# A scheduled attention kernel: a clock for the load queue, normalisation on GpSimd, and a later gate exponential

## The chip, the cores and the metric

The kernel runs on one core of a Trainium2 chip. The metric is the device time of one execution in microseconds (us); lower is better. Times are medians of several executions. All executions count as undisturbed ("fast"). Ratios are computed from the mean time of one kernel's fast runs over that of the other's in the same rounds, so they are not quite the ratio of the medians quoted; the 95% interval stands behind them. The kernel before ran again beside every set of experiments and had medians of 902.8, 902.4, 902.3 and 901.9 us.

The engines' names in the profile are: PE (TensorE, matrix products), PEld (its weight loads), ACT (ScalarE), DVE (VectorE), POOL (GpSimd), SP (SyncE, which here issues the loads and stores). L827 is line 827 of the kernel in question; line numbers differ from kernel to kernel.

## The reference, cut to what matters

Two attention blocks are computed and concatenated, each with 32 heads of 16 columns over 2048 positions (bf16).

```python
# A: four segments of 512 positions, each with causal local attention and a memory
for s in range(4):
    p = softmax(q_s @ k_s^T * scale + causal_mask);  a_dot = p @ v_s
    a_mem = (phi(q_s) @ M) / (phi(q_s) @ z + 1e-6)       # phi(t) = t+1 if t>0 else exp(t)
    o_s = g * a_mem + (1 - g) * a_dot                    # g = sigmoid(beta), one per head
    M += phi(k_s)^T @ v_s;  z += sum(phi(k_s))
# B: full attention over 2048 positions
o = softmax(q @ k^T * scale) @ v
# both: o @ wo
```

The exponentials of the softmax dominate. Block B alone has 32 x 2048 x 2048 of them.

## The kernel before: the parts the change touches

The program is written by a scheduler in Python. It keeps a model clock for each engine (`T["pe"]`, `T["act"]` and so on), picks the next piece of work by these clocks, and pins the order that results. At run time every engine follows its own list in that order; a wait that the model did not foresee holds up everything behind it on that engine (in the kernel before, the copy of kA had its input at 9.03 us and started at 13.13, behind an exponential that waited for a load until 13.02).

Scores go in tiles of three and two banks (512 columns each) to ScalarE's exponential. A part of the score quads (a quad is four score tiles of 512 columns) goes to VectorE instead: four *evacuations* out of PSUM (the accumulator memory) into 16-bit integers that are bit patterns of exponentials, then three *rungs*, which shift a whole quad by a constant within SBUF (the on-chip memory).

```python
# evacuation (PSUM -> SBUF) and rung (SBUF -> SBUF), both on VectorE
nc.vector.tensor_scalar(x[:, j, :], vt[:], XSCALE, float(LADDER[0]), ALU.mult, ALU.add)
nc.vector.tensor_scalar(p[:], x[:], float(off - LADDER[0]), 32767.0, ALU.add, ALU.min)
```

A finished pair of heads is normalised on VectorE. `tT` is the transposed local product, `aT` that of the memory.

```python
def fin_pair(wk, st, name, rt, ridx, ot):
    ...                                      # reciprocals of the sums: rr, r2
    t1, t2 = tT[:, :, :, 0:DH], aT[:, :, :, 0:DH]
    yield -0.7
    pin(nc.vector.tensor_tensor(t1, t1, rr.to_broadcast(bc), op=ALU.mult))
    yield -0.7
    pin(nc.vector.tensor_tensor(t2, t2, r2[:].to_broadcast(bc), op=ALU.mult))
    yield -0.7
    pin(nc.vector.tensor_tensor(o, t1, t2, op=ALU.add))
```

The loads and transposes of x (`xT_a`) and of phi(k) (`phk`) stand in one queue on SP. The scheduler guesses when they will have landed:

```python
rel = T["pe"] + 10                      # projections of segment s > 0 not before this
...
held["pk"] = T["dve"] + 6.5
chore(d - 3, mem(), 2, after=T["dve"] + 7)     # memory products after the transposes of phk
```

The head copies the first keys on ScalarE, behind the gate exponential in program order:

```python
pin(nc.scalar.activation(gcol[:], beta_t[:], ACT.Exp, scale=-1.0))   # needs the load of beta
pin(nc.scalar.copy(kA[0, 0][:], ps0[0][:]))                          # the first scores need kA
```

The tail computes four last output tiles (`l_ps`), checks all sums (`flag`; a branch over an exact fallback follows it), and evacuates the output tiles.

## Time and profile before

The kernel took 902.71 us (902.5 to 904.79, three runs); the profiled run took 901.82 with a span of 900.1 us from its first instruction to its last. From the page of the kernel before, first the busy time of the engines, then the costliest groups of ScalarE and VectorE (line, engine, operation, tiles, shapes, count, then busy us and mean ns of one, then idle time just before and its main releaser):

```profile
PE 866.8 (96%) x7674; PEld 260.2 (29%) x7674; DVE 794.2 (88%) x1359; ACT 868.2 (96%) x779; POOL 152.1 (17%) x327
...
L827 ACT ACTIVATE pT<-s_ps 128x1536 bf16<-128x1536 f32 x749 | 856.8, 1287 | 8.3 <-PE s_ps L109 6.1
L899 DVE TENSOR_SCALAR vx<-v_ps 128x512 uint16<-128x512 f32 x496 | 324.7, 684 | 30.2 <-PE v_ps L109 23.8
...
L915 DVE TENSOR_SCALAR vx<-vx 128x2048 uint16<-128x2048 uint16 x372 | 244.6, 690 | 1.9 <-PE acc L109 0.7
```

TensorE and ScalarE are both busy 96% of the span, but a part of TensorE's work adds nothing to the result (411 products with zeros, busy 137.1 us, which the scheduler puts in as *warming* when TensorE has little to do). ScalarE has nothing of the kind, so it is the bound, and the span divides into what stands before, in and behind its row of exponentials. I read these parts from the start and end of every ScalarE instruction in the trace:

| part of the span, kernel before | us |
|---|---|
| until the first exponential starts | 14.41 |
| ScalarE at work until the last exponential ends (1872 banks) | 864.9 |
| ScalarE idle in the first 20 us after its first exponential | 4.4 |
| ScalarE idle later | 3.2 |
| from the end of the last exponential to the end | 13.1 |

The later idle time is almost nil: in the middle only 3.2 us of some 850 are lost. The head is where time is lost openly. The timeline of the kernel before (start, length, engine, line, operation, count, and in brackets the idle time before it and what ended it):

```profile
9.07 1.41 DVE L1069 TENSOR_SCALAR qA<-q_ps,par 128x512 bf16<-128x512 f32 x2 [6.20 <-PE q_ps L109]
...
13.02 0.21 ACT L1066 ACTIVATE gcol<-beta_t 128x8 f32<-128x8 bf16 x1 [9.66 <-DMA beta_t<-in_A_beta_dram]
13.13 0.57 ACT L1067 CAST kA<-k_ps 128x512 bf16<-128x512 f32 x1
...
14.41 2.37 ACT L827 ACTIVATE pT<-s_ps 128x1536 bf16<-128x1536 f32 x2 [0.71 <-PE s_ps L109]
```

The first projections end at 9.03, but the copy of kA waits behind the gate exponential, which waits for beta until 13.02. And the tail, timeline of the kernel before:

```profile
890.84 0.89 DVE L1165 STREAM_TRANSPOSE OT_b<-tN 128x128 bf16<-128x128 bf16 x4
...
891.65 0.14 DVE L420 TENSOR_SCALAR okt<-rsum 128x32 bf16<-128x32 f32 x1
...
891.85 1.07 ACT L1181 CAST osb<-l_ps 128x512 bf16<-128x512 f32 x2 [4.91 <-PE l_ps L109]
...
892.69 0.14 DVE L1175 TENSOR_SCALAR flag<-f_ps 1x1 int32<-1x1 f32 x1 [0.26 <-PE f_ps L109]
892.76 1.29 DVE L1179 CAST osb<-l_ps 128x512 bf16<-128x512 f32 x2
```

The check of sums runs between 891.65 and 892.83; VectorE's output copies come after it.

### The profile page before, as it was taken

Reading aid. Unit: us, or ns where it says so; the run is one execution under the profiler, and the core shown is the slowest. Engines: PE = TensorE matmul, PEld = TensorE weight load, DVE = VectorE, ACT = ScalarE, POOL = GpSimd, SP = SyncE. Lnnn points to the kernel's source line nnn. Section 1 sums busy time; section 2 is a strip of 40 time slices with the busy share of each in tenths; the row PEclk is TensorE's granted clock in tenths of the full one; section 3 lists DMA queues with packets and bytes.
Section 4 is the critical chain, followed back from the end, with each engine's and each line's share of the span. In section 5 each row is a group of like instructions: output and inputs, shape, how many; then the busy total and the mean of one; then the engine's idle time right before and its main releaser. Section 6 shows DMA issues by size and latency. Waiting matters only on the chain.

```text
span 900.1 us, 18954 instructions
## 1 busy us (share of the span) xinstructions
PE 866.8 (96%) x7674; PEld 260.2 (29%) x7674; DVE 794.2 (88%) x1359; ACT 868.2 (96%) x779; POOL 152.1 (17%) x327
## 2 busy tenths in 40 slices
PE   6999999999999999999999999999999999999996
PEld 2222222232323223222232223223222222222321
DVE  1777789989898998988989999999999899999995
ACT  3899999999999999999999999999999999999994
POOL 4630120411303003030120304002030300000000
PEclk8999999999999999999999999999999999999998
DMA  7700000010000110000000010000000000000001
GB/s 185 143 13 7 24 4 5 7 25 7 7 1 14 36 30 8 1 1 7 1 7 2 25 30 1 1 1 1 2 2 1 19 30 1 2 1 2 1 2 28
DMA packets 35649, 15.47 MB, mean 17 GB/s; under 512 B 27360, under 2 KB 35552, under 8 KB 35552
## 3 DMA queue, kind: packets, MB, share of 16 engines
q1 hardware_dynamic: 33776, 13.78, 6.5%
q8 instruction: 62, 1.02, 0.5%
q10 hardware_dynamic: 1776, 0.40, 0.2%
q14 instruction: 35, 0.29, 0.1%
HBM read 4.20 MB, written 4.19 MB: 9 GB/s over the span
## 4 chain that ended last, share of the span: by engine, by line
PE 42%; ACT 31%; issue 12%; DVE 5%; POOL 2%; DVEq 0%; ACTq 0%; POOLq 0%
ACT pT L827 30%; PE acc L109 19%; PE s_ps L109 11%; PE v_ps L109 7%; POOL pT L837 2%; DVE vx L899 2%; PE o_ps L109 2%; PE k_ps L109 1%; DVE vx L915 1%; ACT ex L284 1%; PE q_ps L109 1%; PE am_ps L109 0%; DVE tT L358 0%; DVE tN L391 0%; POOL qB L259 0%
## 5 line engine op out<-in xcount | busy, mean ns | idle before, releaser
L827 ACT ACTIVATE pT<-s_ps 128x1536 bf16<-128x1536 f32 x749 | 856.8, 1287 | 8.3 <-PE s_ps L109 6.1
L899 DVE TENSOR_SCALAR vx<-v_ps 128x512 uint16<-128x512 f32 x496 | 324.7, 684 | 30.2 <-PE v_ps L109 23.8
L109 PE MATMUL s_ps<-qB,KB 32*128 32x512 bf16 x1552 | 250.7, 382 | 8.9 <-ACT pT L827 5.5
L915 DVE TENSOR_SCALAR vx<-vx 128x2048 uint16<-128x2048 uint16 x372 | 244.6, 690 | 1.9 <-PE acc L109 0.7
L109 PE MATMUL acc<-vx,VB 128*32 128x512 f16 x1984 | 181.3, 385 | 0.6 <-DVE vx L915 0.3
L109 PE MATMUL v_ps<-qB,KB 32*128 32x512 bf16 x496 | 171.4, 382 | 1.1 <-DVE vx L899 0.5
L837 POOL TENSOR_SCALAR_AFFINE_SELECT pT<-pT 128x256 bf16<-128x256 bf16 (+2 forms) x242 | 104.8, 462 | 306.0 <-ACT pT L827 304.7
L109 PE MATMUL acc<-pT,VB 128*32 128x512 bf16 x1552 | 152.8, 387 | 0.0
L109 PEld LDWEIGHTS <-KB 32*128 32x128 bf16 x2048 | 84.2, 91 | 235.8 <-issue 227.8
L109 PE MATMUL acc<-zeros 128*128 128x512 bf16 x411 | 137.1, 386 | 0.0
L109 PEld LDWEIGHTS <-VB 128*32 128x32 bf16 x3536 | 74.5, 94 | 161.7 <-issue 152.4
L109 PE MATMUL s_ps<-qA,kA 32*128 32x384 bf16 (+3 forms) x512 | 54.1, 303 | 7.7 <-ACT kA L1067 4.7
L109 PEld LDWEIGHTS <-zeros 128*128 128x128 bf16 x433 | 35.1, 98 | 84.9 <-issue 77.0
L259 POOL TENSOR_SCALAR qA<-qc,par 128x512 bf16<-128x512 bf16 x24 | 16.5, 701 | 248.6 <-DVE qc L257 248.6
L358 DVE STREAM_TRANSPOSE tT<-acc 128x512 f32<-128x512 f32 x64 | 45.0, 704 | 10.2 <-PE acc L109 9.9
L109 PE MATMUL acc<-pT,vA 128*32 128x256 bf16 (+3 forms) x512 | 32.5, 305 | 1.2 <-DVE vx L899 0.8
L109 PEld LDWEIGHTS <-kA 32*128 32x128 bf16 x512 | 17.1, 92 | 47.8 <-issue 39.7
L259 POOL TENSOR_SCALAR qB<-qc,par 128x512 bf16<-128x512 bf16 x32 | 23.6, 750 | 8.6 <-DVE qc L257 8.6
L435 DVE CAST osb<-o_ps 128x512 bf16<-128x512 f32 x28 | 19.2, 687 | 6.6 <-PE o_ps L109 6.3
L304 DVE CAST vA<-v_ps 128x512 bf16<-128x512 f32 x16 | 11.0, 689 | 11.7 <-PE v_ps L109 11.7
L257 DVE CAST qc<-q_ps 128x512 bf16<-128x512 f32 x28 | 19.2, 684 | 2.4 <-PE q_ps L109 2.1
L109 PE MATMUL k_ps<-xT_a,w_a 128*128 128x512 bf16 x64 | 19.6, 383 | 0.8 <-DMA xT_a<-in_A_x_dram 0.7
(88 smaller groups left out, 419.1 us busy)
## 6 DMA issues: line engine op xcount, KB each, us to landing
out_dram<-osb SPq DMA_DIRECT2D x31, 128.0 KB, 1.7
w_b<-in_B_wqkv_dram SPq DMA_DIRECT2D x3, 512.0 KB, 5.2
phk<-phkT SPq DMA_TRANSPOSE x48, 2.3
w_a<-in_A_wv_dram SPq DMA_DIRECT2D x1, 512.0 KB, 6.6
wo_a<-in_A_wo_dram SPq DMA_DIRECT2D x1, 512.0 KB, 4.3
wo_b<-in_B_wo_dram SPq DMA_DIRECT2D x1, 512.0 KB, 5.1
w_a<-in_A_wk_dram SPq DMA_DIRECT2D x1, 384.0 KB, 7.9
w_a<-in_A_wq_dram SPq DMA_DIRECT2D x1, 384.0 KB, 8.5
```

Source lines behind the costliest of these rows:

```text
L109: return pin(nc.tensor.matmul(out, lhsT, rhs, **k))
L257: pin(nc.vector.tensor_copy(qc[:], ps[:]))
L259: pin(nc.gpsimd.tensor_scalar(dst[:, e, :], qc[:], par[:, e:e + 1], 0.0, ALU.mult, ALU.add))
L284: pin(nc.scalar.activation(ex[:], src, ACT.Exp))
L304: pin(nc.vector.tensor_copy(dst, ps[:].rearrange("p (h d) -> p h d", d=DH)))
L358: pin(nc.vector.transpose(st["tT"][:, e].rearrange("p c d -> p (c d)"), acc[:]))
L435: pin(nc.vector.tensor_copy(osb[:], ps[:]))
L827: pin(nc.scalar.activation(pT[:, 0:n, :], pt[:, 0:n, :], ACT.Exp, scale=SCALE))
L837: pin(nc.gpsimd.affine_select(out=blk, in_=blk, compare_op=ALU.is_ge, fill=0.0, base=0, pattern=[[0, len(sls)], [1, P]], channel_multiplie ...
L899: pin(nc.vector.tensor_scalar(x[:, j, :], vt[:], XSCALE, float(LADDER[0]), ALU.mult, ALU.add))
L915: pin(nc.vector.tensor_scalar(p[:], x[:], float(off - LADDER[0]), 32767.0, ALU.add, ALU.min))
```

## The change

Six parts, all in the scheduler:

1. **Head.** Weight slices for the second row tile are loaded first; beta comes in one contiguous load behind the weights and is spread by four GpSimd copies; the gate exponential moves behind six score tiles.
2. **A clock for the load queue.** `T["sp"]` counts the queued transfers, and the releases of projections and memory products go by it.
3. **Normalisation on GpSimd.** The large `tensor_tensor` operations are offered to GpSimd, if possible beside evacuations of VectorE rather than beside its rungs.
4. **Limits.** `VBACK` 1.5 to 1.8 and a new `VLATE` steer how many quads VectorE takes; `KLEAD=3` releases keys of block B earlier.
5. **Tail.** Two of the last partial products come earlier, and the output tiles are evacuated before the check of sums.
6. A guard on the buffer of `aT`, needed by part 3.

```diff
-VBACK = 1.5
+VLATE = 0.5
+VBACK = 1.8
+KLEAD = 3
-    T = dict(pe=0.0, act=0.0, dve=0.0, pool=0.0)
+    T = dict(pe=0.0, act=0.0, dve=0.0, pool=0.0, sp=SPLOADS)
+    def on_sp(us, ready):
+        T["sp"] = max(T["sp"], ready) + us
...                                                     # in fin_pair, three times
-            yield -0.7
-            pin(nc.vector.tensor_tensor(t1, t1, rr.to_broadcast(bc), op=ALU.mult))
+            eng = (yield (POOLTT, 0.7)) or nc.vector
+            pin(eng.tensor_tensor(t1, t1, rr.to_broadcast(bc), op=ALU.mult))
...                                                     # in pool_run
+            while ptasks and max(T["pool"], ptasks[0][0]) < T["pe"] + 0.15:
+                free = sum(t["us"] for t in runnable() if not t["port"] and t["ready"] < T["pe"] + 0.3)
+                if live[0] and free < POOLWITH and T["pe"] < ptasks[0][0] + POOLWAIT:
+                    return                              # wait for evacuations to run beside
+                ready, us, f = ptasks.popleft()
+                on_pool(us, ready)
+                f()
...
-                rel = T["pe"] + 10
+                rel = T["sp"] + 3.5
...
-                held["pk"] = T["dve"] + 6.5
+                held["pk"] = T["sp"] + 2.0
-                chore(d - 3, mem(), 2, after=T["dve"] + 7)
+                chore(d - 3, mem(), 2, after=T["sp"] + 2.5)
...                                                     # head
-        pin(nc.scalar.activation(gcol[:], beta_t[:], ACT.Exp, scale=-1.0))
         pin(nc.scalar.copy(kA[0, 0][:], ps0[0][:]))
...
-                if t == 3:
-                    later(1.2, gates, prio=1)
+                if t == 6:
+                    pin(nc.scalar.activation(gcol[:], beta_t[:], ACT.Exp, scale=-1.0))
+                    later(1.2, gates, prio=1, ready=on_act(0.2, T["pe"]))
...                                                     # tail
-        while len(pvq) > 1:
+        while len(pvq) > TAILPV:                        # TAILPV = 2
             assert pv(1, True)
```

Because a scheduler decides, the built programs differ in more than the diff shows: VectorE gets two more quads (504 evacuations instead of 496, 378 rungs instead of 372), so ScalarE has 1864 banks instead of 1872; 29 normalisation operations land on GpSimd; the warming products with zeros fall from 411 to 376.

## The prediction

> **What bounds it now.** ScalarE's softmax exponentials. The page has ACT 868.2 of 900.1 us; groups by form: 374 exponentials of 1536 columns and 375 of 1024, 856.8 us together for 1872 banks of 512 columns. The windows view has ACT at 97 to 100% from 30 to 880 us. So span = start of the first exponential (14.41 us, timeline) + ACT work (about 865) + ACT idle in between (about 4.2 up to 30 us, 3.4 after) + tail after the last exponential (886.94 to 900.1 = 13.2).
>
> **The head.** The first projections end at 9.05, but the ACT copy of kA starts only at 13.13: in program order it stands behind the gate exponential, which waits 9.7 us for the beta load (waits view). The scores wait 4.7 us for kA, and the clock falls to 0.61. The change moves that exponential behind six score tiles and loads beta contiguously; the copy should start at about 9.1, first scores 9.85, first exponential at 10.4 to 10.5: -3.9 us, all critical. Weight slices for row tile 1 come first, so its projections stand ready early.
> Against it: the spreading of beta sits on GpSimd ahead of the ones of V and of the causal masks, and beta is now queued behind 1.28 MB of weights (before, these landed at 15.7). I expect beta at 15 to 16.5, masks from about 17, first product with V at about 18.3, while six tiles run out at 17.4: one ACT hole of about 2 us near 17.4 to 19.5. Early idle about 2.7 instead of 4.2: -1.5.
>
> **The middle.** The instruction order of the built kernels has two more score quads on VectorE (496 to 504 evacuations, 372 to 378 rungs), so 1864 banks on ACT (746 instructions). Fit to the trace: 0.081 us each plus 0.425 per bank; 8 banks and 3 instructions are 3.6 us, critical. 29 normalisation operations (0.66 to 0.78 us on VectorE) move to GpSimd: -20 us of VectorE, +9.7 us for the added quads; VectorE stays near 785 us, not the bound. GpSimd +29 x about 1.2 = 35 us (estimate; its bf16 128x512 takes 0.70), idle enough. 35 warming matmuls less are worth nothing by themselves. [...] rungs (SBUF to SBUF) have median 684, maximum 1009 ns, evacuations from PSUM at most 693; GpSimd's copies reach 1646 with median 695. The change places the GpSimd work beside evacuations, so I expect rungs a little slower, hardly any on the ACT chain: idle after 30 us stays 2 to 5.
>
> **The tail.** Evacuation comes before the check of sums: last output 1.1 us earlier, but the flag about 1.3 later, and the branch is followed by about 3.5 us anyway: +0.3. Two partial products move ahead of the last PVs: +0.5. Total +0.8.
>
> **Sum.** -3.9 -1.5 -3.6 +0.8 = -8.2: 902.7 becomes about 894.5 us, range 889.5 to 899.5. Faster by over 2%: 0.03; within 2%: 0.94; slower: 0.03.
>
> **What would show it.** First exponential at 10.5 (not 14.4), no wait on beta in ACT, clock near 1 in 10 to 20 us; a hole near 18 with GpSimd releasing; exponentials 746, busy about 853; DVE about 785, POOL about 190; idle after 30 us unchanged; tail 13 to 15 us.
>
> **What would make it wrong.** Beta or V weights landing later (a longer hole) or much earlier (no hole: 892); GpSimd operations of 2 us or more that hold back transposes, accumulators and masks in their in-order queues (new holes, up to 900); a VectorE so relieved that ACT idle after 30 us vanishes (891).

The 1.2 us per operation on GpSimd is the scheduler's own constant (`POOLTT`); measured, GpSimd's busy time rose by 35.8 us (152.1 to 187.9).

## The result

The changed kernel took 909.48 us (908.37 to 911.05, four runs) against 902.79 (902.5 to 904.79, four runs): ratio 1.0071 [1.005, 1.0092]. It is slower by 0.7%, within 2%, and 15 us above the predicted time.

From the page of the kernel after, the lines that answer to those shown of before:

```profile
PE 866.5 (95%) x7661; PEld 260.8 (29%) x7661; DVE 794.3 (87%) x1344; ACT 866.4 (95%) x776; POOL 187.9 (21%) x359
...
L866 ACT ACTIVATE pT<-s_ps 128x1536 bf16<-128x1536 f32 x746 | 855.3, 1288 | 20.4 <-PE s_ps L118 16.5
L939 DVE TENSOR_SCALAR vx<-v_ps 128x512 uint16<-128x512 f32 x504 | 329.6, 683 | 27.6 <-PE v_ps L118 22.8
L955 DVE TENSOR_SCALAR vx<-vx 128x2048 uint16<-128x2048 uint16 x378 | 259.2, 716 | 1.0
...
L118 PE MATMUL acc<-vx,VB 128*32 128x512 f16 x2016 | 185.5, 388 | 4.7 <-DVE vx L955 3.6
```

Three things stand out. ScalarE's idle time before exponentials grew from 8.3 to 20.4 us, and the part of it that scores ended from 6.1 to 16.5. The rungs became dearer, 690 to 716 ns on average. And TensorE now waits for rungs: 3.6 us before products with `vx`, against 0.3 before.

The same division of the span as before, from the profiled runs (span 907.8 us):

| part of the span | before | after | after − before | predicted |
|---|---|---|---|---|
| until the first exponential | 14.41 | 10.01 | −4.4 | −3.9 |
| ScalarE idle, first 20 us | 4.4 | 2.8 | −1.6 | −1.5 |
| ScalarE at work | 864.9 | 863.3 | −1.6 | −3.6 |
| ScalarE idle later | 3.2 | 16.7 | **+13.5** | 0 |
| tail | 13.1 | 15.0 | +1.9 | +0.8 |
| sum | 900.1 | 907.8 | +7.8 (rounded parts) | −8.2 |

The head came out as intended. Timeline of the kernel after:

```profile
8.55 0.58 ACT L1113 CAST kA<-k_ps 128x512 bf16<-128x512 f32 x1 [5.22 <-PE k_ps L118]
...
10.01 6.88 ACT L866 ACTIVATE pT<-s_ps 128x1536 bf16<-128x1536 f32 x6 [0.87 <-PE s_ps L118]
...
21.20 1.02 ACT L866 ACTIVATE pT<-s_ps 128x1024 bf16<-128x1024 f32 x1 [2.41 <-PE s_ps L118]
```

The predicted hole of about 2 us is there (2.41 us before 21.20); what makes it was not tested, and in the kernels of experiments 3, 9 and 10 it is only 1.1 to 1.3 us long. So the loss is in the middle, which the prediction had taken as unchanged. The windows view shows where; its columns are window, length, busy time (and instructions) of PE, PEld, DVE, ACT and POOL, then PEclk, the granted TensorE clock (1.00 is full), the DMA share and GB/s. Kernel before:

```profile
200.00:250.00 50.00, 48.37 (x417) 15.16 (x413) 42.81 (x76) 50.00 (x48) 11.59 (x23) 1.00 0.03 7
...
650.00:700.00 50.00, 49.26 (x462) 14.68 (x458) 47.76 (x81) 49.74 (x45) 8.66 (x18) 1.00 0.00 1
```

Kernel after:

```profile
200.00:250.00 50.00, 46.90 (x401) 14.54 (x398) 39.84 (x70) 46.79 (x44) 12.64 (x25) 0.97 0.04 8
...
650.00:700.00 50.00, 48.11 (x411) 13.18 (x407) 42.85 (x71) 45.23 (x40) 10.71 (x19) 0.90 0.00 1
```

In the first window ScalarE lost 3.2 us (46.79 instead of 50.00), in the second 4.5 us, and in both the granted clock fell. The trace has two stretches with a granted clock of 0.50 in the middle of the kernel after, at 203.4 to 206.8 and 674.4 to 684.6 us, and none in that of before. ScalarE's idle time within 3 to 4 us of these adds up to 7.95 of the 16.7 us; the rest lies in small gaps. All four timed runs have a mean clock of 0.987 or 0.988, so the stretches are not peculiar to the profiled one. What came just before each stretch differs.

**Near 203 us: the load queue.** Timeline of the kernel after (SPq is SP's queue of transfers):

```profile
191.37 4.98 SPq L235 DMA_TRANSPOSE xT_a<-in_A_x_dram  x3
...
196.46 5.24 SPq L331 DMA_TRANSPOSE phk<-phkT  x4
...
201.75 1.26 SPq L235 DMA_TRANSPOSE xT_a<-in_A_x_dram  x1
203.16 0.21 PE L118 MATMUL m_ps<-vA,phk 128*128 128x68 bf16 x1 [1.34 <-DMA phk<-phkT]
...
203.99 1.02 ACT L866 ACTIVATE pT<-s_ps 128x1024 bf16<-128x1024 f32 x1 [1.59 <-PE s_ps L118]
204.05 1.90 PE L118 MATMUL k_ps<-xT_a,w_a 128*128 128x512 bf16 x4
...
206.60 2.37 ACT L866 ACTIVATE pT<-s_ps 128x1536 bf16<-128x1536 f32 x2 [1.58 <-PE s_ps L118]
```

The transposes of x and of phi(k) stand back to back in one queue. The memory products (`m_ps`) were released by the new clock too early. TensorE works in order, so scores wait behind them: 1.34 us here, 1.67 with the smaller wait just before. At a clock of 0.50 the next four projections take 1.90 us, where every other row of four in this trace takes 1.04, and ScalarE runs dry twice (1.59 and 1.58 us). The clock fell after 1.67 us of idle time of TensorE in the 3.4 us before (the length of this stretch at 0.50). In the 3.4 us before the other stretch, at 674.4, it was 1.21 us. In the 3.4 us from 618.78 to 622.19 it was 1.25 us, and the clock stayed at 1.00: about as much idle time stands before a drop and before none. What tells these places apart was not found.

**Near 670 us: normalisation on GpSimd beside rungs.** Timeline of the kernel after:

```profile
669.84 1.05 POOL L417 TENSOR_TENSOR tT<-tT,r 128x512 f32<-128x512 f32 x1 [2.05 <-DVE r L404]
...
670.16 2.75 DVE L955 TENSOR_SCALAR vx<-vx 128x2048 uint16<-128x2048 uint16 x2
...
670.86 1.50 POOL L419 TENSOR_TENSOR aT<-aT,r 128x512 f32<-128x512 f32 x1
...
671.50 0.40 PE L118 MATMUL acc<-vx,VB 128*32 128x512 f16 x4 [0.47 <-DVE vx L955]
...
672.96 0.40 PE L118 MATMUL acc<-vx,VB 128*32 128x512 f16 x4 [0.75 <-DVE vx L955]
...
673.79 1.45 ACT L866 ACTIVATE pT<-s_ps 128x1536 bf16<-128x1536 f32 x1 [0.94 <-PE s_ps L118]
```

Two rungs take 2.75 us here, where two take 1.29 in the kernel before (at 880.48). Products of TensorE need them and wait 0.47 and 0.75 us; the scores behind those come late (ScalarE idles 0.94 us), the clock drops to 0.50 at 674.4, and ScalarE idles again. That these waits brought the clock down is read from the order in time; no run tests it.

Which rungs are slow shows when all rungs are paired with the GpSimd work they overlap, over the whole trace of the kernel after:

| VectorE operation | beside a normalisation on GpSimd | beside no GpSimd work |
|---|---|---|
| rung (SBUF to SBUF) | 23, mean 1.13 us | 333, mean 0.68 us |
| evacuation (PSUM to SBUF) | 18, mean 0.67 us | 432, mean 0.68 us |

Rungs take longer beside a normalisation (1.13 against 0.68 us), evacuations do not (0.67 against 0.68). GpSimd's operations take longer too. On GpSimd a multiplication (into `tT`, `aT`, or `tN` from one product) takes 1.05 to 1.10 us in this trace, and 1.5 when it starts inside a rung, or inside one of VectorE's large instructions with two inputs in SBUF (`phq`, `phkT`). The sum (`tN<-tT,aT`) takes 1.6 us inside a rung, as all six do here, and 1.28 in the kernel of experiment 8 where it starts beside an evacuation. The groups by form mix these cases (kernel after):

```profile
L417 POOL TENSOR_TENSOR tT<-tT,r 128x512 f32<-128x512 f32 x12 | 13.5, 1127 | 24.7 <-DVE r L404 24.7
L419 POOL TENSOR_TENSOR aT<-aT,r 128x512 f32<-128x512 f32 x7 | 10.1, 1446 | 0.0
L421 POOL TENSOR_TENSOR tN<-tT,aT 128x512 bf16<-128x512 f32 x6 | 9.6, 1594 | 11.9 <-DVE aT L419 11.8
```

So the scheduler's wish "beside evacuations" was granted in part only: 23 rungs still ran beside a normalisation. The extra time of these rungs is about 23 x (1.13 − 0.68) = 10.4 us.

Two theories stood after this reading. *The first (mine): the operations moved to GpSimd slow the rungs beside them, TensorE waits for rungs, and ScalarE starves; the new load-queue clock adds one stall; the tail adds 2 us.* *The rival: the slower rungs are harmless, and the middle is slow because the whole order of instructions is a worse one (fewer warming products, two more quads, other release times).* A smaller rival asks for what the data dependence costs, that is VectorE waiting for GpSimd's results. The waits view of the kernel after shows no such wait of any size, so I took it as excluded. "The theory" in the expectations below is the first of the two.

### The profile page after: what moved, and what is told of

Read it like the earlier page. It is cut to its first block, busy times and chain, and to the rows that moved or that the text cites. A ratio compares the mean times of both kernels' runs of the same rounds, so it can differ in the third digit from the quotient of the medians.

```text
span 907.8 us, 18900 instructions
## 1 busy us (share of the span) xinstructions
PE 866.5 (95%) x7661; PEld 260.8 (29%) x7661; DVE 794.3 (87%) x1344; ACT 866.4 (95%) x776; POOL 187.9 (21%) x359
## 5 line engine op out<-in xcount | busy, mean ns | idle before, releaser
L866 ACT ACTIVATE pT<-s_ps 128x1536 bf16<-128x1536 f32 x746 | 855.3, 1288 | 20.4 <-PE s_ps L118 16.5
L939 DVE TENSOR_SCALAR vx<-v_ps 128x512 uint16<-128x512 f32 x504 | 329.6, 683 | 27.6 <-PE v_ps L118 22.8
L955 DVE TENSOR_SCALAR vx<-vx 128x2048 uint16<-128x2048 uint16 x378 | 259.2, 716 | 1.0
L118 PE MATMUL acc<-vx,VB 128*32 128x512 f16 x2016 | 185.5, 388 | 4.7 <-DVE vx L955 3.6
L118 PE MATMUL v_ps<-qB,KB 32*128 32x512 bf16 x504 | 180.7, 384 | 3.2 <-DVE vx L939 2.5
L118 PE MATMUL acc<-zeros 128*128 128x512 bf16 x376 | 130.0, 390 | 0.0
L118 PEld LDWEIGHTS <-VB 128*32 128x32 bf16 x3560 | 77.4, 94 | 173.1 <-issue 162.8
L375 DVE STREAM_TRANSPOSE tT<-acc 128x512 f32<-128x512 f32 x64 | 44.6, 701 | 15.9 <-PE acc L118 15.8
L118 PEld LDWEIGHTS <-zeros 128*128 128x128 bf16 x396 | 32.6, 98 | 81.1 <-issue 75.6
L409 POOL TENSOR_TENSOR tN<-tT,rsum 128x512 bf16<-128x512 f32 x3 | 3.2, 1054 | 121.5 <-DVE rsum L398 121.5
L275 POOL TENSOR_SCALAR qB<-qc,par 128x512 bf16<-128x512 bf16 x32 | 22.1, 704 | 16.1 <-DVE qc L273 16.1
L273 DVE CAST qc<-q_ps 128x512 bf16<-128x512 f32 x28 | 19.2, 685 | 4.4 <-PE q_ps L118 2.6
L320 DVE CAST vA<-v_ps 128x512 bf16<-128x512 f32 x16 | 11.0, 690 | 12.4 <-PE v_ps L118 12.3
```

The lines of the kernel that those rows point to most:

```text
L118: return pin(nc.tensor.matmul(out, lhsT, rhs, **k))
L273: pin(nc.vector.tensor_copy(qc[:], ps[:]))
L275: pin(nc.gpsimd.tensor_scalar(dst[:, e, :], qc[:], par[:, e:e + 1], 0.0, ALU.mult, ALU.add))
L320: pin(nc.vector.tensor_copy(dst, ps[:].rearrange("p (h d) -> p h d", d=DH)))
L375: pin(nc.vector.transpose(st["tT"][:, e].rearrange("p c d -> p (c d)"), acc[:]))
L409: pin(eng.tensor_tensor(o, tT[:, :, :, 0:DH], rr.to_broadcast(bc), op=ALU.mult))
```

## The experiments

Twelve kernels ran, each with correct output except one. All were timed, with one profiled run each. In three sets, each had its own runs of the kernel before on the same chip.

### 1. Normalisation back on VectorE, at the same places

The scheduler plans as in the kernel after, as if for GpSimd; only the engine in the instruction differs. The orders of TensorE and ScalarE are identical to those of the kernel after.

```diff
                     if T["pool"] < T["pe"] + POOLSLACK and len(ptasks) < 2:
-                        on[0] = nc.gpsimd
+                        on[0] = nc.vector
```

> The changed kernel with the 29 normalisation operations issued on VectorE at the very places where they were issued on GpSimd; the scheduler's own clocks are left as they were, so the instruction order on TensorE and ScalarE is identical, instruction for instruction. Theory [...]: longest rung back from 1768 to about 1000 ns, rung mean from 716 to about 690, no clock drop near 674, ScalarE idle after 290 us down from about 9 to 2-4 us, time 903 to 905 (from 909.5). Rival 'VectorE too full / schedule too tight' (more quads, later limits for backlog): the 20 us put back on VectorE make things no better, time 908 to 913.

Measured: 908.29 us, 1.0051 [1.003, 1.0073] of the kernel before; later idle time of ScalarE 15.7 us. The time lies in the range that the expectation gave to the rival, not in that of the first theory. The longest rung did come back, from 1.77 to 1.10 us, and no clock drop stands near 674; but one stands at 624 to 631 (a clock in the 0.8s in that slice of the page), and that near 204 stayed. The gain that faster rungs should have brought did not come: 1.2 us between the medians, which the noise can make (906.2 us at a mean clock of 0.994 to 909.4 at 0.989 in the four runs). The page of this kernel says why:

```profile
PE 868.8 (96%) x7661; PEld 260.0 (29%) x7661; DVE 798.5 (88%) x1373; ACT 867.0 (96%) x776; POOL 150.8 (17%) x330
...
L955 DVE TENSOR_SCALAR vx<-vx 128x2048 uint16<-128x2048 uint16 x378 | 248.7, 688 | 1.0
```

The rungs are back at 688 ns, but VectorE has 29 operations more. In the same order of everything else, VectorE is busy 798.5 us with them and 794.3 us with them on GpSimd. The five groups of large normalisation operations add up to 39.0 us here and to 19.2 us in the kernel after, so 19.8 us of work left VectorE, and 4.2 us of busy time did (7.2 by the sum of all durations; busy time counts overlapping records once). Most of the difference is the rungs (259.2 − 248.7 = 10.5 us). The order was made for a VectorE without this work, and in neither kernel did it have that VectorE. TensorE's waits show what took the place of the slow rungs: from the kernel after to this one, those for rungs fell from 3.6 to 0.55 us, and those for evacuations rose from 4.9 to 6.5. So the engine alone is not the cause. Whether the work at these places or the order as such starves ScalarE stayed open, since one load was put in place of another; experiment 5 was added for that.

### 2. A wider margin behind the load queue

```diff
-                chore(d - 3, mem(), 2, after=T["sp"] + 2.5)
+                chore(d - 3, mem(), 2, after=T["sp"] + 5.0)
```

> The changed kernel, with the memory product released 5.0 instead of 2.5 us after the modelled end of the load queue (the schedule from about 190 us on is rearranged by it: a new arrangement of equal quality). Theory 'queue clock too early': TensorE no longer waits 1.7 us for the transposed phi(K) near 202, the clock drop at 203 to 207 and the two ScalarE gaps of 1.6 us vanish: about -3 us at that place, 905 to 908 in all if the rest is like before. Rival 'chance of one arrangement': such waits appear at another segment, time 908 to 911.

Measured: 904.6 us, 1.0016 [0.9999, 1.0033]; later idle 13.5 us. It is about 5 us better than the kernel after, but in the profiled run the stall did not vanish; it moved. Now `k_ps` waited 1.76 us for `xT_a`, and the clock fell at 205.5 to 212.3 (in the 0.8s in that slice of the page), with 3.9 us of idle time of ScalarE around it. That run was the slowest of the four (907.1 us, mean clock 0.990); two others have a mean clock of 0.994, as the kernel before has, so the drop probably did not come in each. The scheduler also made another program of it (1868 banks on ScalarE), so a part of the gain may come from that. A fixed margin on one release alone is no cure while the other release stays early.

### 3. The head alone, on the kernel before

The head's edits are those of the diff above (loads, spreading of beta, gate exponential behind tile 6, arrival times), put into the kernel before.

> The kernel before with only the head of the change (row tile 1 of the weights loaded first, beta in one load behind them, gate exponential behind six score tiles, arrival times). If the head is worth what the trace of the changed kernel shows up to 30 us (first exponential 4.4 us earlier, 1.5 us less idle): 896 to 898.5. If an earlier start only makes later stages run out of data or the order chaotic: 899 to 903.

Measured: 903.33 us, 1.0004 [0.9987, 1.0021]: no gain. The first exponential did start early (10.97 instead of 14.41) and the early idle time fell from 4.4 to 1.6 us. But ScalarE's work rose by 3.8 us (1876 banks instead of 1872, as the scheduler gave VectorE one quad less; at 462 ns a bank, four banks are an estimated 1.8 us of it), the later idle time by 3.4 and the tail by 0.8. These parts sum to −3.4 − 2.8 + 3.8 + 3.4 + 0.8 = +1.8, as the spans have it (901.8 against 900.1). The microseconds won at the start were given back later.

### 4. The tail alone, on the kernel before

```diff
+TAILPV = 2
-        while len(pvq) > 1:
+        while len(pvq) > TAILPV:
             assert pv(1, True)
...     # the check of sums (sums_ok ... flag) moves from before to behind the output evacuations
```

> The kernel before with only the tail of the change (two partial products ahead of the last two products with V; outputs evacuated before the check of the sums). All order before the tail is identical. My prediction put +0.8 us on it; the two traces show the stretch from the last exponential to the end grown by 1.84 us, part of which comes from another mix of work at the end. Expect 903.3 to 904.5; if the tail is harmless, 902.5 to 903.

Measured: 905.9 us, 1.0027 [1.001, 1.0045], more than expected. From the end of the last exponential to the end it takes 15.54 us instead of 13.14: +2.4. (The rest of this profiled run's difference lies before the first exponential, +1.65, and in the 20 us behind it, +0.84: beta happened to land 1.6 us later, which the edit does not touch.) The timeline of the kernel with the new tail alone:

```profile
894.06 0.89 DVE L1171 STREAM_TRANSPOSE OT_b<-tN 128x128 bf16<-128x128 bf16 x4
...
895.75 1.29 DVE L1178 CAST osb<-l_ps 128x512 bf16<-128x512 f32 x2 [0.81 <-ACT osb L1180]
...
896.96 0.17 DVE L421 TENSOR_SCALAR okt<-rsum 128x32 bf16<-128x32 f32 x1
...
898.02 0.15 DVE L1189 TENSOR_SCALAR flag<-f_ps 1x1 int32<-1x1 f32 x1 [0.26 <-PE f_ps L110]
```

From the start of the transposes to the end of the flag it now takes 898.17 − 894.06 = 4.1 us; before it was 892.83 − 890.84 = 2.0. Before, the check ran in a gap in which VectorE had to wait for its output tiles anyway. Now VectorE idles in that gap (0.81 us, waiting for ScalarE's copy), copies for 1.3 us, and only then starts the check. The branch behind the flag ends the program: some 7 us from flag to end in both kernels (7.3 before, 6.8 here). Here the last output lands 6.3 us before the end, so the flag is critical and the last output is not. In the kernel before the two are close: the last output lands only 2.1 us before the end, and SP issues it just before it takes the branch. Another 0.65 us comes from the partial products, which now stand ahead of the last products with V (last exponential to first transpose 3.9 before, 4.55 here). Together 2.1 + 0.65 − 0.4 is the 2.4 measured.

### 5. Neither on GpSimd nor on VectorE

The order of the kernel after, with the moved operations cut to one sixteenth of their columns, or replaced by a zero fill on VectorE where their result had to be whole. The result is wrong (relative error 13.7), the orders of TensorE and ScalarE are identical to those of the kernel after.

```diff
             eng = (yield (POOLTT, 0.7)) or nc.vector
-            pin(eng.tensor_tensor(t1, t1, rr.to_broadcast(bc), op=ALU.mult))
+            n = 1 if eng is nc.gpsimd else 16
+            pin(eng.tensor_tensor(t1[:, :, 0:n], t1[:, :, 0:n], rr[:, :, 0:n].to_broadcast([P, 2, n, DH]), op=ALU.mult))
...     # the same for t2; for the last, o: nc.vector.memset(tN[:], 0.0) if eng is nc.gpsimd
```

> A wrong result on purpose: the changed kernel, in which the 29 GpSimd normalisation operations are cut to nothing (19 of them to a sixteenth of their size on GpSimd, 10 replaced by a fill of zeros on VectorE). The order on TensorE and ScalarE is again identical, instruction for instruction. [...] If late rungs [...] cause the idle of ScalarE after 290 us: its idle there falls from 9 to 2-4 us, no clock drop near 674, 901 to 904. If the order of TensorE's instructions as such starves ScalarE: it stays, 906 to 910. The stall near 202 (transposed phi(K)) and the tail should stay in either case.

Measured: 896.56 us, 0.9933 [0.991, 0.9956], so 12.9 us less than the kernel after, with the same order of instructions, and below the expected range. Between the two profiled runs it is 10.9 us, of which 8.3 are later idle time. That is now 8.4 us, half of it (4.2) at the stall near 201, which this kernel keeps. The rungs of this kernel (page), and the place near 670 us, which here lies at 664 (timeline):

```profile
PE 862.0 (96%) x7661; PEld 260.5 (29%) x7661; DVE 783.9 (87%) x1354; ACT 864.4 (96%) x776; POOL 158.6 (18%) x349
...
L963 DVE TENSOR_SCALAR vx<-vx 128x2048 uint16<-128x2048 uint16 x378 | 248.7, 689 | 1.0
```

```profile
664.83 0.24 POOL L421 TENSOR_TENSOR tT<-tT,r 128x32 f32<-128x32 f32 x1 [2.06 <-DVE r L404]
...
665.15 1.27 DVE L963 TENSOR_SCALAR vx<-vx 128x2048 uint16<-128x2048 uint16 x2
665.31 0.56 POOL L424 TENSOR_TENSOR aT<-aT,r 128x32 f32<-128x32 f32 x1 [0.25 <-DVE r L417]
```

Two rungs take 1.27 us instead of 2.75, and neither the waits of TensorE nor a clock drop follow. TensorE waits 2.4 us in all for rungs and evacuations, against 8.5 in the kernel after, 7.0 in experiment 1 and 3.3 in the kernel before. This speaks against the rival: the order as such does not starve ScalarE. (That the time is below that of the kernel before says little, since this kernel does less work.) What it cannot bear is the moved work itself, on GpSimd beside rungs as little as on VectorE. The two runs together (1 and 5) say what the moved operations cost VectorE: 794.3 − 783.9 = 10.4 us of VectorE's time with the operations on GpSimd, 798.5 − 783.9 = 14.6 with them on VectorE (this kernel has 10 zero fills of 0.27 us of its own, so each figure is some 2.7 us too low).

### 6. More warming products

A rival for the clock drops: 35 warming products fewer. `WARMTH` 0.52 to 0.62 gives 562 instead of 376.

```diff
-WARMTH = 0.52
+WARMTH = 0.62
```

> The changed kernel with more warming matmuls (threshold 0.62 instead of 0.52; 562 instead of 376 of them). If the clock drops (3.4 and 10.2 us at half speed) come from too few warming matmuls: no drop, ScalarE idle near them (8 us) gone, 902 to 905. If they only follow from stalls of TensorE, drops can remain or the extra work costs as much as it saves: 907 to 911.

Measured: 924.57 us, 1.0249 [1.0221, 1.0278], slower by 15 us than the kernel after (907 to 911 were expected), and still with clock drops (568 to 571 and 687 to 691; the window from 650 to 700 has a mean clock of 0.97). Later idle time rose to 24.7 us. ScalarE's work rose too, from 863.3 to 871.6 us; the reason was not looked for. So more warming products do not prevent the drops. Nor are 35 fewer the reason for them: the kernels of experiments 9 to 11 have only 336 or 333 and no drop in the middle. The rival falls.

### 7. The old limits for quads

```diff
-VLATE = 0.5
-VBACK = 1.8
+VLATE = 0.0
+VBACK = 1.5
```

> The changed kernel with the old limits for handing quads to VectorE (backlog 1.5 instead of 1.8, no extra minimum under backlog); the number of quads stays 126, only their places differ. If the raised backlog limit is what packs VectorE too tightly: 903 to 906. If not: 908 to 911, the same as the changed kernel.

Measured: 904.3 us (903.3 to 905.72 in four runs, 913.18 in the fifth, which was the profiled one; its mean granted clock was 0.977, that of the others 0.988 to 0.990), 1.0022 [0.9997, 1.0047]. The number of evacuations and rungs stays 504 and 378, so the two added quads come not from the limits but from VectorE looking free. The profiled run had four clock drops, one of 17 us (in the page one slice of 22.8 us has a granted clock in the 0.6s), and 15.4 of its 21.1 us of later idle time lie near them; what its undisturbed runs look like inside is not known. But four of the five runs are some 5 us faster than the kernel after, in the range that the expectation gave to the raised limit as a cause, although 29 normalisation operations are still on GpSimd and 21 rungs run beside them (mean 1.13 us). So the limits may be a second cause, or this is the luck of another arrangement: experiment 2 changed only a margin and won as much. The runs do not tell these apart.

### 8. Normalisation on GpSimd alone, on the kernel before

Parts 3 and 6 of the change (the engine choice in `fin_pair`, the queue in `pool_run`, the guard on `aT`) put into the kernel before; head, load-queue clock, limits and tail stay old.

> The kernel before with only the normalisation part of the change (30 operations go to GpSimd, the scheduler then gives VectorE two more quads, 496 to 504 evacuations). My prediction had -3.6 us for this part. The theory now [...]: no gain, idle of ScalarE after 30 us up from 3.2 to 8 us or more, 902 to 907. If the harm is in other parts: 898 to 901.

Measured: 914.92 us (913.53 to 919.47), 1.0154 [1.0117, 1.0191]. This part, with the two added quads and the new order that the scheduler makes of it, costs 12.6 us, more than expected. The later idle time is 15.9 us against 3.2, with no clock drop in the profiled run; 1864 banks on ScalarE, and 22 rungs beside a normalisation with a mean of 1.15 us. TensorE waits 17 times for rungs, 7.4 us in all. From the page of this kernel:

```profile
L937 DVE TENSOR_SCALAR vx<-vx 128x2048 uint16<-128x2048 uint16 x378 | 259.5, 717 | 2.0 <-PE acc L113 0.7
L113 PE MATMUL acc<-vx,VB 128*32 128x512 f16 x2016 | 186.3, 385 | 8.1 <-DVE vx L937 7.4
```

So the loss needs no clock drop and nothing of the other parts. No kernel moved the operations to GpSimd without adding the two quads, so the shares of the two are not told apart.

### 9 and 10. A version that keeps what pays

From these: the kernel after, but never normalising on GpSimd (the scheduler knows it), with the tail of before, and with both rules for a release, the later of the two.

```diff
-                rel = T["sp"] + 3.5
+                rel = max(T["sp"] + 3.5, T["pe"] + 10)
-                chore(d - 3, mem(), 2, after=T["sp"] + 2.5)
+                chore(d - 3, mem(), 2, after=max(T["sp"] + 2.5, T["dve"] + 7))
-                    if T["pool"] < T["pe"] + POOLSLACK and len(ptasks) < 2:
+                    if False:
...     # and the tail of the kernel before
```

> The changed kernel without its three faults by the theory: normalisation never on GpSimd (and the scheduler knows it: 496 evacuations, as before), the tail of before (check of the sums in VectorE's gap, last products with V ahead of one partial product), and the memory product and the loads released no earlier than both the old and the new rule say. Head, limits for VectorE and arrival times stay those of the change. If the theory accounts for the loss: head worth 5 to 6 us against before, idle after 30 us 3 to 6 us, tail 13 to 13.5, no clock drop: 896 to 899. If the earlier start is eaten by TensorE and VectorE having the same work in less time: 900 to 903.

The second version also spreads beta behind the causal masks of the first three tiles on GpSimd:

```diff
-        spread_beta()
...
                 t += 1
+                if t == 3:
+                    spread_beta()
+                    on_pool(0.9, 14.3)
```

> As c1, with the spreading of beta on GpSimd moved behind the causal masks of the first three score tiles instead of ahead of all (the order on TensorE is the same). If the hole of 2.4 us near 19 us comes from masks that stand behind the beta load: the hole is gone, 1.5 to 2.4 us faster than c1. If it comes from late V weights: equal to c1.

Measured: 897.4 us, 0.995 [0.9932, 0.9968], and 897.04 us (896.88 to 897.22), 0.9941 [0.9924, 0.9958]. Both beat both kernels, by about 5 and 12 us, and neither has a clock drop in the middle of its profiled run. They take three parts back at once and have an arrangement of their own, so they show a version that works and not what each part is worth. The groups of the second version (page):

```profile
L866 ACT ACTIVATE pT<-s_ps 128x1536 bf16<-128x1536 f32 x749 | 856.0, 1292 | 8.0 <-PE s_ps L118 4.8
...
L955 DVE TENSOR_SCALAR vx<-vx 128x2048 uint16<-128x2048 uint16 x372 | 247.1, 692 | 2.0 <-PE acc L118 0.5
```

ScalarE's wait before exponentials is back from 20.4 to 8.0 us. TensorE still waits 4.7 us for rungs and evacuations (3.1 of it for rungs, 8.5 in all in the kernel after), so the sum of these waits alone does not set the time. By parts (second version against before): start 10.81 instead of 14.41, early idle 1.4 instead of 4.4, work 865.0 instead of 864.9, later idle 5.7 instead of 3.2, tail 12.3 instead of 13.1. The two windows shown above, second version:

```profile
200.00:250.00 50.00, 47.71 (x412) 15.05 (x417) 43.56 (x78) 50.00 (x47) 14.08 (x25) 1.00 0.06 12
...
650.00:700.00 50.00, 47.20 (x443) 14.69 (x449) 43.96 (x75) 49.95 (x45) 7.78 (x17) 1.00 0.01 1
```

ScalarE is full in both and the clock is 1.00. The place of the spreading made no difference that could be measured (1.55 against 1.43 us of early idle time). But the hole was down to 1.2 us already in the first version, so this does not test where the 2.4 us in the kernel after came from.

### 11. The old kernel with the head and the later spreading

```diff
+                if t == 3:                             # on the kernel of experiment 3
+                    spread_beta()
+                    on_pool(0.9, 14.3)
```

> The kernel before with only the head of the change (as b_head, 903.3) and beta spread behind the first three masks. b_head lost the 6 us of its head again: 4 banks more on ScalarE, 3.4 us more idle, 0.8 more tail. Expect 901 to 903; if a different arrangement by chance, down to 899.

Measured: 902.85 us, 1.0012 [0.9987, 1.0037]. As in experiment 3 the head alone gains nothing. The early idle time is 1.4 us, but there are again 1876 banks and a later idle time of 6.6.

### 12. The best version with the old limits and no earlier keys

```diff
-VLATE = 0.5
-VBACK = 1.8
+VLATE = 0.0
+VBACK = 1.5
-KLEAD = 3
+KLEAD = 0
```

> As c2, with the old limits for VectorE (backlog 1.5, no extra minimum) and without the earlier projection of keys: 500 evacuations, 2 banks of 1024 less on ScalarE. If one more quad for VectorE pays (4 banks, about 1.8 us): 894 to 897; if VectorE is full: 898 to 902.

Measured: 914.03 us, 1.0135 [1.0117, 1.0154], 17 us slower than the version it derives from and outside both expected ranges. ScalarE idles 22.1 us in the middle. The longest single gap, 3.6 us before 177.2, stands behind ten projections of keys nearly in a row and a wait of TensorE of 1.38 us for a rung; no clock drop goes with it. The profile shows waits for keys: 2.1 us for `KB` near 115 us, 2.9 us in four waits of `k_ps` for `xT_a` from 193 to 198. A clock drop goes with each of these two places (116 to 119 and 194 to 204; the window from 200 to 250 has a mean clock of 0.96). So some of these three numbers are needed with the early start. Since all three changed at once, the runs do not say which; the wait for `KB` points to `KLEAD`.

## Why the prediction was wrong, point by point

**The bound: right.** ScalarE's row of exponentials bounds the kernel, and the five parts of the span added up in every run.

**The head: right.** Predicted −3.9 and −1.5, measured −4.4 and −1.6 within the changed kernel; a hole of about 2 us was there too, though its cause was not tested. What the prediction did not say is that an earlier start is no gain by itself: alone it brought nothing (experiments 3 and 11), and the time came back as more banks and more idle time on ScalarE. Whether it pays depends on the arrangement that follows.

**The middle: wrong; this step failed.** The prediction said "I expect rungs a little slower, hardly any on the ACT chain: idle after 30 us stays 2 to 5". It had seen single rungs of up to 1009 ns beside a median of 684 in the trace of the kernel before, and then priced slower rungs at nothing. It took the GpSimd work to run beside evacuations, but 23 rungs ran beside it. Measured, the later idle time rose from 3.2 to 16.7 us. Most of that goes with the moved normalisation. With the two quads that follow from it, it cost 12.6 us alone (experiment 8). Its removal from the same order gave 12.9 us and took the later idle time from 16.7 to 8.4 us, of which 4.2 belong to the load queue (experiment 5). It is the work at these places, in an order planned for a VectorE without it, and not GpSimd as such: put back on VectorE in the same order, it starved ScalarE as much (15.7 us, experiment 1). Two errors went into it. First, the relief was counted from operations: 20 us off VectorE. The same order with either engine shows a relief of 4.2 us (798.5 to 794.3), since the rungs take 10.5 us more beside GpSimd's work (259.2 against 248.7 us). Second, the two added quads were taken as paid for by that relief. They cost an estimated 9.7 us of VectorE (eight evacuations and six rungs at the durations of the kernel before), so VectorE's busy time stayed where it was, 794.2 and 794.3, and now with single rungs up to 2.6 times as long (1.77 us), at moments when TensorE waits for them. How much of the idle time each error made is not separated. The prediction compared sums ("VectorE stays near 785 us, not the bound"). An engine that is not the bound can still hold up the one that is, by one late result at a time (near 673 us two late rungs, and ScalarE idle for 0.94 us).

**The load-queue clock: not considered.** The prediction did not price part 2 at all. It released memory products before their transposes had landed, which cost about 3 us near 203 in the profiled run. With the later of the old and the new rule the stall did not occur (experiments 9 and 10); moving one margin alone only moved it in the profiled run (experiment 2).

**ScalarE's work: half the size.** Predicted −3.6 for eight banks, measured −1.6. The work comes to 463.1 ns a bank in the kernel after and 462.0 before. In the records an exponential overlaps the one before it by 0.143 us on average in the kernel before and by 0.141 in the kernel after, which has more gaps between them; that is about 1.3 us in all. Removing banks and adding gaps partly cancel.

**The warming products: "worth nothing by themselves" stands.** More of them made it worse (experiment 6). But the prediction looked for clock drops in the head only, and two came in the middle, behind short waits.

**The tail: right in direction, size off.** Predicted +0.8; measured +1.9 in the kernel after and +2.4 alone (experiment 4). The later flag was put at +1.3 with most of it hidden behind the branch; measured it is +2.1, and little hides it (0.4 us), since the branch waits for the flag and the end comes about 7 us behind it.

**The counts were near:** 746 exponentials busy 855.3 us (about 853 predicted), GpSimd 187.9 (about 190), the tail 15.0 (13 to 15). VectorE's 794.3 (about 785) looks near too, but its 9 us too many are about what the rungs lost beside GpSimd. The sums hid the error; the order in time shows it.

**What stays open.** No kernel had large GpSimd operations at these places without any tie to VectorE's data, so that was not tried. That GpSimd's work slows the rungs is thus shown by overlap (1.13 against 0.68 us) and by experiments 1 and 5 (mean rung 688 and 689 ns instead of 716), not by a load on GpSimd alone; by what mechanism, no run shows. In experiment 1 the operations took 4 us more of VectorE and yet the kernel was no slower; the 1.2 us between the two are within the noise. The added quads were never run without the move, nor the move without them. Experiments 2 and 7 won 5 us with small changes of the order while the normalisation stayed on GpSimd, so the size of the loss depends on the arrangement. Which of the three numbers makes experiment 12 slow, and why the early start alone costs four banks, was not told apart. Other arrangements than the twelve were not searched.

## What to carry to other kernels

Before moving work to an idle engine, look in a trace for what the operations of the engine to be relieved take beside such work (here a rung took 1.13 us beside a normalisation on GpSimd and 0.68 without), and price the relief by the time the relieved engine is busy in the same order, not by the operations removed: here 19.8 us of operations moved and 4.2 us of busy time were saved. Where an order is fixed in advance, judge each planned release by the slowest of its sources (the larger of two estimates here), because one early instruction that must wait holds up all behind it; near 203 us here, the granted TensorE clock fell to 0.50 right after such a wait (1.34 us). At the end of a program, find out which result ends it before moving things around it; here, with the new tail, it was the flag and not the output.
